# Finishing the norms of k apart from those of q in a kernel's opening, and loading the root's table behind the first loads

## The chip, the cores and the metric

One core of one Trainium2 chip runs the whole program. The metric is device time in microseconds (us) of one execution, median of several runs. Engines: PE is TensorE (matmuls; PEld is its weight load, which overlaps), DVE is VectorE, ACT is ScalarE, POOL is GpSimd, SP is SyncE.

## The reference

Two operators, one after the other, on B=4, N=6080, C=256 and 2048 hidden columns; float32 in and out.

```python
def _attn_ref(q, k, v, tau):                       # tau = 1
    qn = q / (np.linalg.norm(q, axis=1, keepdims=True) + 1e-06)
    kn = k / (np.linalg.norm(k, axis=1, keepdims=True) + 1e-06)
    s = kn.transpose(0, 2, 1) @ qn / tau           # 256 x 256 per batch
    s = s - s.max(-1, keepdims=True)
    a = np.exp(s)
    a /= a.sum(-1, keepdims=True) + 1e-09
    return v @ a

def _moe_ref(x, w_in, w_out, s, b):                # x = the result above, 24320 x 256
    h = x @ w_in
    r = np.maximum(h, 0.0)
    g = s * (r * r) + b
    return g @ w_out
```

The inputs are random normals (q, k, v times 0.1).

## The kernel before

For each batch the kernel needs s = kᵀq over all 6080 rows and the column norms of k and q before it can form the softmax a. It then folds the softmax into the weights, wa = a · w_in, so that the long part is only v · wa, the squared relu, and the product with w_out. For batches 1 to 3 the k and q work is spread over the long part of the batch ahead. For batch 0 there is nothing to hide behind: the **opening** (the first 39 us) loads k and q, and only after their last rows come the norms, the scaling of s, its transposes, the exponentials (eT), the sums, the folding of the weights (wa), and then the first steady matmul (h_ps). The change touches this opening alone.

The parts that the argument needs (cuts marked; the comments are added here):

```python
class Gram:                                     # one per batch
    def load(self, c):                          # chunk c of k, then of q
        ...
        for i, src in enumerate((k, q)):
            rows = src[self.b, at : at + np_ * jc, :].rearrange("(p j) c -> p j c", j=jc)
            ...                                 # first two chunks: SP and ACT queues
            po(nc.gpsimd.dma_start(out=t[:np_, i, :jc, :], in_=rows))
    ...
    def add_norms(self, last=False):            # sums of squares of k and q, one tile
        ...
    def finish_ops(self):
        def norms():
            self.add_norms(last=True)
            po(nc.scalar.activation(out=nrm, in_=self.n_ps, func=AF.Sqrt))
        def recip():                            # DVE: + EPS, reciprocal
        def scale():                            # DVE: sm_s = s_ps * 1/|k|
        def turn():                             # PE: t_ps = transpose(sm_s)
        def ready(func):                        # a one-column activation, brings the table
            po(nc.scalar.activation(out=warm, in_=ones32[:, 0:1], func=func))
        def exps(j):                            # ACT: eT = exp(t_ps * 1/|q|), halves j = 0, 1
        def sums():                             # PE: r_ps = column sums; DVE: rs = 1/r_ps
        def scaled(f0, n, m, wa_ps):            # m = 0 on ACT, m = 1 on DVE
            dst = self.wa[:, m, ds(f0, n)]
            if m == 0:
                po(nc.scalar.mul(out=dst, in_=wa_ps, mul=st["rs"][:, m : m + 1]))
            else:
                po(nc.vector.tensor_scalar_mul(
                    out=dst, in0=wa_ps, scalar1=st["rs"][:, m : m + 1]))
        ...

    # the opening, in program order
    nc.vector.memset(parts16, 1.0 / LAM)
    nc.vector.memset(ones32, 1.0)
    ...
    po(nc.scalar.activation(out=warm, in_=ones32[:, 0:1], func=AF.Sqrt))   # root's table, at once
    ...                                         # loads: k, q, k, q, ... k, q; then w_in, v, w_out
    for c in range(NCH0):                       # per chunk: norm sums, s_ps matmuls, squares
        ...
    fin = g0.finish_ops()
    fin[1](); fin[2](); fin[3](); fin[4]()      # norms, recip, scale, ready(Exp)
    keep_busy(4, w_in16[:, 0, :P], w_in16[:, 0, :NW])     # filler matmuls
    fin[5]()                                    # turn
    transpose_v(0)                              # PE transposes of v, copied by DVE
    for f in fin[6:12]:                         # exps 0 and 1, sums, first folds of the weights
        f()
```

`po` fixes the order of the instructions of an engine as written.

## Time and profile before

| | kernel before |
|---|---|
| time, median (lowest to highest) | 719.46 us (719.45 to 719.73), 3 runs |
| profiled span, granted clock | 717.6 us, 1.0 |
| PE busy | 699.5 us, 97% |
| last shares of k and of q land | 34.11 and 34.30 us |
| first exponential (eT) starts | 37.32 us |
| first and second steady matmul (h_ps) start | 39.28 and 39.50 us |

A line of the timeline reads: start in us, busy us, engine, source line, operation, output tile <- input tiles, their shapes, xcount for a group; in brackets the idle time of the engine just before it, and which engine or transfer ended that idle time. The prediction below shows the lines up to the exponentials. These are the ones behind them, from the timeline of the kernel before:

```profile
38.48 0.17 DVE L297 RECIPROCAL rs<-r_ps 128x2 f32<-128x2 f32 x1
38.75 0.88 ACT L302 ACTIVATE wa<-wa_ps,rs 128x256 f16<-128x256 f32 x2 [0.59 <-PE wa_ps L309]
38.94 0.92 DVE L304 TENSOR_SCALAR wa<-wa_ps,rs 128x256 f16<-128x256 f32 x2 [0.29 <-PE wa_ps L309]
39.28 0.60 PE L605 MATMUL h_ps<-vT,wa 128*128 128x512 f16 x2
```

ACT scales one half of the folded weights and DVE the other. Each of the first two steady matmuls needs one of these halves. DVE waits 0.29 us between its reciprocal and its first scaling, and the second half is there in time: the two h_ps matmuls are one group without a gap.

### The profile page before, as it was taken

Reading aid. Unit: us, or ns where it says so; the run is one execution under the profiler, and the core shown is the slowest. Engines: PE = TensorE matmul, PEld = TensorE weight load, DVE = VectorE, ACT = ScalarE, POOL = GpSimd, SP = SyncE. Lnnn points to the kernel's source line nnn. Section 1 sums busy time; section 2 is a strip of 40 time slices with the busy share of each in tenths; the row PEclk is TensorE's granted clock in tenths of the full one; section 3 lists DMA queues with packets and bytes.
Section 4 is the critical chain, followed back from the end, with each engine's and each line's share of the span. In section 5 each row is a group of like instructions: output and inputs, shape, how many; then the busy total and the mean of one; then the engine's idle time right before and its main releaser. Section 6 shows DMA issues by size and latency. Waiting matters only on the chain.

```text
span 717.6 us, 17642 instructions
## 1 busy us (share of the span) xinstructions
PE 699.5 (97%) x7481; PEld 505.1 (70%) x7481; DVE 626.0 (87%) x879; ACT 544.4 (76%) x588; POOL 110.1 (15%) x189
## 2 busy tenths in 40 slices
PE   4799999999999999999999999999999999999998
PEld 3556777776677777777677777777668777777777
DVE  4779999998789999999888899999887888888886
ACT  4489877887777777788777778778877777777875
POOL 4532332201201222111110222110000000000000
PEclk9999999999999999999999999999999999999999
DMA  9999897647556879443972877944423333321201
GB/s 236 207 259 169 158 177 134 111 108 129 115 103 121 144 133 145 107 93 78 157 154 56 143 136 124 152 93 84 107 63 75 93 71 74 97 59 46 83 30 74
DMA packets 89790, 84.25 MB, mean 117 GB/s; under 512 B 59664, under 2 KB 64848, under 8 KB 89712
## 3 DMA queue, kind: packets, MB, share of 16 engines
q0 software_dynamic: 26064, 43.40, 37.2%
q1 hardware_dynamic: 63072, 38.43, 21.4%
q8 instruction: 58, 0.95, 0.6%
q10 hardware_dynamic: 576, 1.31, 0.5%
q14 instruction: 20, 0.16, 0.1%
HBM read 78.91 MB, written 24.90 MB: 145 GB/s over the span
## 4 chain that ended last, share of the span: by engine, by line
PE 93%; DMA 4%; DVE 1%; ACT 1%; POOL 0%; issue 0%; ACTq 0%; POOLq 0%
PE h_ps L605 45%; PE o_ps L773 40%; PE s_ps L142 4%; PE wa_ps L309 2%; DMA qk<-in_q_dram 2%; DMA qk<-in_k_dram 1%; DMA w_in<-in_moe_w_in_dram 1%; PE o_ps L677 1%; PE o_ps L651 0%; ACT r L615 0%; POOL qk L126 0%; PE idle_ps L442 0%; DVE o_sb L633 0%; DVE S L701 0%; DVE sq L162 0%
## 5 line engine op out<-in xcount | busy, mean ns | idle before, releaser
L615 ACT ACTIVATE r<-h_ps 128x1024 f16<-128x1024 f32 (+1 forms) x384 | 387.6, 1013 | 146.2 <-PE h_ps L605 144.3
L605 PE MATMUL h_ps<-vT,wa 128*128 128x512 f16 (+7 forms) x1632 | 452.0, 364 | 0.1
L773 PEld LDWEIGHTS <-S 128*128 128x128 f16 x2944 | 198.0, 98 | 84.8 <-issue 0.4
L773 PEld LDWEIGHTS <-g 128*128 128x128 f16 x2208 | 155.1, 98 | 74.1
L628 DVE TENSOR_TENSOR g<-r 128x2048 f16<-128x2048 f16 (+2 forms) x150 | 174.7, 1165 | 14.6 <-ACT r L615 14.5
L773 PE MATMUL o_ps<-T,S 128*128 128x128 f16 x2208 | 183.3, 219 | 0.1
L605 PEld LDWEIGHTS <-wa 128*128 128x128 f16 x1632 | 136.1, 98 | 20.6 <-DVE wa L304 0.2
L773 PE MATMUL o_ps<-w_out,g 128*128 128x128 f16 x1472 | 134.2, 219 | 0.2 <-DVE u L633 0.2
L633 DVE SCALAR_TENSOR_TENSOR o_sb<-o_ps,s_out,u 128x256 f32<-128x256 f32 x138 | 66.4, 481 | 47.4 <-PE o_ps L773 44.9
L626 ACT ACTIVATE g<-r 128x1024 f16<-128x1024 f16 (+1 forms) x97 | 100.4, 1035 | 0.2
L142 PE MATMUL s_ps<-qk 128*128 128x256 f16 (+1 forms) x384 | 70.1, 283 | 13.9 <-ACT qk L133 8.8
L361 POOL DMA_DIRECT2D v<-in_v_dram x48 | 31.4, 658 | 262.4 <-DMA vT<-v 199.1
L633 DVE SCALAR_TENSOR_TENSOR u<-o_ps,s_out,rowconst 128x256 f32<-128x256 f32 x138 | 65.9, 477 | 0.0
L773 PE MATMUL o_ps<-w_out,S 128*128 128x128 f16 x736 | 63.4, 219 | 0.0
L773 PE MATMUL o_ps<-N,g 128*128 128x128 f16 x736 | 63.4, 219 | 0.0
L188 POOL DMA_DIRECT2D f<-f x30 | 26.4, 879 | 225.6 <-DVE f L178 172.0
L165 ACT ACTIVATE sq<-qk 128x1024 f16<-128x1024 f16 (+3 forms) x49 | 50.4, 1033 | 11.7 <-DMA qk<-in_k_dram 7.8
L701 DVE TENSOR_TENSOR S<-S,g 128x2048 f16<-128x2048 f16 (+1 forms) x47 | 56.4, 1201 | 1.3
L699 DVE TENSOR_TENSOR S<-g 128x2048 f16<-128x2048 f16 (+1 forms) x47 | 56.1, 1193 | 0.0
L705 DVE TENSOR_TENSOR S<-g,S 128x2048 f16<-128x2048 f16 x46 | 55.9, 1215 | 0.0
L703 DVE TENSOR_TENSOR S<-g 128x2048 f16<-128x2048 f16 x46 | 55.9, 1215 | 0.0
L142 PEld LDWEIGHTS <-qk 128*128 128x128 f16 (+1 forms) x384 | 32.8, 101 | 19.9 <-DVE qk L132 8.2
(75 smaller groups left out, 324.4 us busy)
## 6 DMA issues: line engine op xcount, KB each, us to landing
out_dram<-o_sb SPq DMA_DIRECT2D x46, 512.0 KB, 3.1
v<-in_v_dram POOLq DMA_DIRECT2D x47, 256.0 KB, 4.7
qk<-in_k_dram POOLq DMA_DIRECT2D x42, 256.0 KB, 5.9
qk<-in_q_dram POOLq DMA_DIRECT2D x42, 256.0 KB, 7.3
f<-f POOLq DMA_DIRECT2D x30, 128.0 KB, 3.0
vT<-v SPq DMA_TRANSPOSE x182, 3.2
w<-in_moe_w_out_dram POOLq DMA_DIRECT2D x4, 512.0 KB, 10.8
raw<-in_k_dram SPq DMA_DIRECT2D x2, 512.0 KB, 6.4
```

Of the source, the lines that this page charges most:

```text
L142: po(nc.tensor.matmul(self.s_ps[:, ch, :], kc[:np_, j, ts(ch, P)], qc[:np_, j, :], start=(c == 0 and j == 0 and ch == 0), stop=(c == len(s ...
L165: po(nc.scalar.activation(out=st["sq"][:np_, 1, js, :], in_=kc[:np_, js, :], func=AF.Square))
L605: po(nc.tensor.matmul(dst, wa[:, ci, ts(m, P)], src, start=(ci == 0), stop=(ci == CH - 1), skip_group_check=True))
L615: po(nc.scalar.activation(out=r16[:, :, i % 2, :n], in_=h_tiles.pop((g, i))[:, :, :n], func=AF.Relu))
L626: po(nc.scalar.activation(out=dst, in_=src, func=AF.Square))
L628: po(nc.vector.tensor_mul(dst, src, src))
L633: po(nc.vector.scalar_tensor_tensor(out=dst, in0=src, scalar=s_out, op0=ALU.mult, in1=add, op1=ALU.add))
L699: po(nc.vector.tensor_add(T[1], A21, A22))
L701: po(nc.vector.tensor_sub(T[2], T[1], A11))
L703: po(nc.vector.tensor_sub(T[3], A11, A21))
L705: po(nc.vector.tensor_sub(T[4], A12, T[2]))
L773: po(nc.tensor.matmul(st[name][:, j, :], a()[:, i, ts(j, P)], w[:, i, :], start=first, stop=last, skip_group_check=True))
```

## The change

Its stated intent: keep the norms of k and q apart, load the last k rows ahead of the last q rows, so that the root and the reciprocal of k are done before q has landed and the scaling of s need not wait for them; and load the root's table "once the first rows of k are there instead of at once". The core of the diff:

```diff
-            self.rows, self.n_ps = [], None
-        def load(self, c):
+            self.raw, self.rows, self.n_ps = {}, ([], []), [None, None]
+        def load(self, c, parts=(0, 1)):
 ...
-            def norms():
-                self.add_norms(last=True)
-                nrm = sm_pool.tile([P, 2, CH], FP32, tag="nrm", name="nrm")
-                po(nc.scalar.activation(out=nrm, in_=self.n_ps, func=AF.Sqrt))
+            def norms(a=None):
+                ...                             # batches 1 to 3: both at once, as before
+                else:
+                    self.add_norms((a,), last=True)
+                    po(nc.scalar.activation(out=st["nrm"][:, a], in_=self.n_ps[a], func=AF.Sqrt))
 ...
-                front += [scale, lambda: ready(AF.Exp), turn]
+                front = [lambda: norms(1), lambda: recip(1), lambda: norms(0),
+                         lambda: ready(AF.Exp), scale, lambda: recip(0), turn]
 ...
-    warm = consts.tile([P, 1], FP32)
-    po(nc.scalar.activation(out=warm, in_=ones32[:, 0:1], func=AF.Sqrt))
     for c in range(NDIRECT):
         g0.load(c)
+    warm = consts.tile([P, 1], FP32)
+    po(nc.scalar.activation(out=warm, in_=raw32[:, 0, 0, 0, 0:1], func=AF.Sqrt, scale=0.0))
 ...
-    for c in range(NDIRECT, len(g0.chunks)):
+    for c in range(NDIRECT, len(g0.chunks) - 2):
         g0.load(c)
+    for parts in ((0,), (1,)):                  # last two chunks: k, k, then q, q
+        for c in range(len(g0.chunks) - 2, len(g0.chunks)):
+            g0.load(c, parts)
 ...
-    FILL = {-9: 2, -8: 2, -7: 2, -6: 4, -5: 4, -4: 4, -3: 4, -2: 1}
+    NFILL = 3
+    FILL = {-9: 2, -8: 2, -7: 2, -6: 4, -5: 4, -4: 4, -3: 2}
 ...
-    fin[4]()
-    keep_busy(4, w_in16[:, 0, :P], w_in16[:, 0, :NW])
-    fin[5]()
-    transpose_v(0)
-    for f in fin[6:12]:
+    ...                                         # squares and norms of k, 3 fillers, then q
+    for f in fin[2:6]:
+        f()
+    fin[6]()
+    transpose_v(0)
+    keep_busy(2, w_in16[:, 0, :P], w_in16[:, 0, :NW])
+    for f in fin[7:13]:
         f()
```

(In the index `a`, 1 is k and 0 is q. The sizes of the loads are as before: the last two chunks put two rows on each of 128 and of 96 partitions; only their order changes.)

## The prediction

> **What bounds the kernel now.** I read four views: the page's busy shares, the chain of waits that ended last, the timeline of the first 62 us, and the trace's landing records (a time for each of the 16 shares in which a transfer reports). The page first:
>
> ```profile
> span 717.6 us, 17642 instructions
> PE 699.5 (97%) x7481; PEld 505.1 (70%) x7481; DVE 626.0 (87%) x879; ACT 544.4 (76%) x588; POOL 110.1 (15%) x189
> ```
>
> TensorE works for 699.5 of 717.6 us. The change touches nothing of that: it edits the opening, before the steady work on v. So the question is how early the opening lets the first steady matmul start. The chain there (start us, us, what):
>
> ```profile
> 27.33 8.14 DMA w_in<-in_moe_w_in_dram
> 35.47 0.05 issue
> 35.52 1.04 PE idle_ps L442 x4
> 36.55 0.74 PE t_ps L272 x4
> 37.30 0.02 issue
> 37.32 0.85 ACT eT L282 x2
> 38.17 0.05 issue
> 38.22 0.23 PE r_ps L292 x3
> 38.44 0.90 PE wa_ps L309 x8
> ```
>
> After 35.47 us no DMA is on this chain, and TensorE, ACT or DVE links follow each other to the end. What the exponentials (eT) gain or lose should therefore reach the end nearly whole. The chain names the w_in landing, but the timeline shows something as late beside it (start us, us, engine, line, operation, out<-in; in brackets the idle time and its releaser):
>
> ```profile
> 34.20 0.63 ACT L165 ACTIVATE sq<-qk 96x512 f16<-96x512 f16 x1 [2.02 <-DMA qk<-in_k_dram]
> 34.33 0.42 DVE L162 TENSOR_TENSOR sq<-qk 96x512 f16<-96x512 f16 x1 [1.22 <-DMA qk<-in_q_dram]
> 34.35 0.60 PE L142 MATMUL s_ps<-qk 96*128 96x256 f16 x4 [0.39 <-DMA qk<-in_q_dram]
> 34.81 0.38 PE L217 MATMUL n_ps<-ones,sq 96*128 96x1 f16 x8
> 35.22 0.17 ACT L228 ACTIVATE nrm<-n_ps 128x4 f32<-128x4 f32 x1 [0.39 <-PE n_ps L217]
> 35.41 1.28 ACT L277 ACT_TABLE_LOAD   x1
> 35.92 0.88 DVE L243 TENSOR_SCALAR sm_s<-s_ps,rnrm 128x256 f32<-128x256 f32 x2
> 36.71 0.20 ACT L277 ACTIVATE warm<-ones 128x1 f32<-128x1 f32 x1
> 37.32 0.84 ACT L282 ACTIVATE eT<-t_ps,rnrm 128x256 f16<-128x256 f32 x2 [0.41 <-PE t_ps L272]
> ```
>
> Two branches leave the last landing (34.30 us): the data branch (norms, root, reciprocal, scale, transposes) ends at 37.30; the table branch (root, then the exponential's table) ends at 36.91. The exponentials wait for the later. The 0.41 us of idle ACT before eT is the lead of the table branch, and so the most that shortening the data branch alone can give.
>
> **What the Trainium skill says.** "ScalarE: Activation LUTs", section "What ACT_TABLE_LOAD costs", has about 1283 ns for the load and about 1380 ns of drain, for every change of set. The trace agrees on the load (1.28 us at both places above and below) but not on a drain here: the next activation starts at 36.71, 0.02 us after the load's end. I use 1.28.
> "DMA: Bandwidth & Descriptors", section "Why a DMA increments its semaphore by 16 and not by 1", says a transfer counts as landed only when all its engines have reported. The landing records agree: the last k transfer (96 rows) has its first share at 32.32 and its last at 34.11; the last q transfer 32.81 and 34.30.
> "Runtime: NRT & Kernel Launch", section "Instruction fetch mechanics", says a sequencer refills instructions by its own DMA queue in 16 KiB blocks. The trace agrees: a 16384-byte packet of the instruction queue runs from 32.08 for 0.96 us, just where one of the 16 shares starts to lag. So that fetch makes the last q rows late, not q itself.
> "TensorE: Matmul & The Clock Gate", section "The HAM clock gate", warns of idle gaps near 3 us. In this trace TensorE, once started, idles 1.85 us at most (at 10.62, still in the warm-up), and the granted clock is 1.00 in every stretch; I expect no change.
>
> **The change part by part.**
> *The root's table.* The diff makes the first root read the first rows of k. The compiled order shows the load of the table ahead of that root without a wait of its own; only the activation waits. The kernel before has these lines:
>
> ```profile
> 1.19 1.28 ACT L401 ACT_TABLE_LOAD   x1 [1.19 <-PEq L846]
> 2.48 0.20 ACT L401 ACTIVATE warm<-ones 128x1 f32<-128x1 f32 x1
> 5.81 1.04 ACT L133 CAST qk<-raw 128x1024 f16<-128x1024 f32 x1 [3.12 <-DMA raw<-in_q_dram]
> ```
>
> So the load will not do what the description says. It moves only behind the second issue of q, 1.19 to some 1.6 us, and still ends near 2.9. The root (0.20) moves to the landing of k (5.61), ends near 5.84 and delays the cast at 5.81 by 0.03 to 0.05. That delay dies: TensorE catches up with the loads at 15.8 us and waits for each later one. Worth 0.0.
> *Order of the last four loads.* k, q, k, q becomes k, k, q, q, with the same bytes on the same queue, so the last q should again land at 34.30. The second-last k loses a q of 128 rows ahead of it (0.65 us from one landing to the next) and gets ahead of the fetch: 31.46 + 0.49 = 31.95 instead of 34.11. The first of the two q takes its place behind the fetch: between 33.5 and 34.1 instead of 32.15.
> *Norms of k alone, early.* ACT squares the two k tails from 31.54 (0.63) and, once DVE has freed the buffer by its fold that ends at 32.31, from 32.36 to 32.99. The sums follow (8 small matmuls, 0.38, partly beforehand) to 33.3, the root of k to 33.5, two DVE steps (0.17 and 0.18, with gaps) to 33.9. All of it is before the q rows; none is on the path any more. That takes root and reciprocal off the data branch.
> *Data branch after.* Last q 34.30; if the other q came only at 34.1, the matmuls of both end at 35.15; otherwise at 34.95. DVE squares both q tails (0.42 each) until 34.8 to 35.0. Scaling starts at 35.0 to 35.2 instead of 35.92 and takes 0.88. Transposes end 0.5 after it (before: 36.80 to 37.29): 36.4 to 36.6, instead of 37.30. Gain on this branch 0.7 to 0.9.
> *Table branch after.* Sums of q still need the last q square: 35.19 if the first q is in time, 35.4 if it is 0.2 behind. Root 0.17, load 1.28, warm 0.20, gaps 0.03 each: 36.93 to 37.14. This is now the later branch, so the exponentials start there: 0.18 to 0.39 earlier than 37.32.
> *Added and moved work.* One more root (0.17) and two more DVE instructions (some 0.35 together) for separate norms; they lie in waits, since the reciprocal of q comes after the scale, with ACT still loading its table. Four transposes of t no longer follow four filler matmuls on w_in. Then v: its first tile lands at 36.70, so its transposes run from 36.75 to 37.4 (before 37.01 to 37.73), two fillers go to some 37.8, and the copy of v on DVE ends at 38.2 (before 38.46). The sums r_ps come after the second exponential, 37.8 to 38.0 plus 0.05. None of these is later than the exponentials by more than 0.1.
> *Sum.* Start of the weights' folding 0.18 to 0.39 earlier; less up to 0.1 where v's copy or the fillers are last. Middle 0.28: 719.46 - 0.28 = 719.18, say 719.2.
>
> **Rivals.** (1) *The fetch hits the early k.* It follows TensorE's own progress, whose order is unchanged up to the block of norm sums, and it starts 0.5 us after the k tail would be through, so I think it misses. If it came 0.5 us earlier, k would land at about 33.5. As DVE takes k's reciprocal ahead of the q squares, these would slip to about 35.9, the table branch to 37.75, and the time would be 719.9. (2) *The data branch stays last,* because scaling waits for something that I overlook, such as a bank or the copy of v: then up to 0.1 of gain or none, 719.4. For it: the chain names PE and DVE there; against: all releases that I find are early. (3) *The early gain is absorbed later*: between 52.6 and 57.4 ACT sets the pace, and between 64.8 and 73.8 DVE does. Both are backlogs that begin after the exponentials, so they should shift along; only if a load of w_out or the next k set them would the gain vanish (719.5). The w_out pieces land by 48.0, well ahead. (4) *TensorE cools* because three fillers are gone: it would cost a microsecond or more; the remaining gaps, under 0.5 us, speak against it. (5) *The table is really held back* until 5.61: then the first cast of q is 1.5 late and the end is still unmoved, since TensorE waits for loads from 15.8.
>
> **Range and chances.** Three runs of the kernel before span 0.28 us, another chip may differ as much, and DMA timing later in the kernel can move some tenths. Together with rivals (1) and (3) on the slow side and a full 0.4 plus luck on the fast side: 718.7 to 719.8. Two per cent is 14 us; the whole opening that is touched is about 3 us long. So within 2% is all but sure: 0.99, the rest split evenly.
>
> **What would show it.** In the changed profile: the first table load at about 1.6, not at 5.6; the last q tail near 34.3, the k tails by 32.0; the root of k near 33.4 and of q at 35.2 to 35.45; scaling from 35.0 to 35.2; ACT idle before eT gone, with eT right behind the warm activation at 36.9 to 37.15; the steady matmuls 0.2 to 0.4 earlier and the same shift still there at 100 us. I am wrong if the k tail lands after 33, if eT still waits for the transposes, if the shift at 100 us differs from the one at 40, or if a matmul of 512 columns in the opening takes visibly longer than its 379 ns.

## The result, and the profile after

| | before | after |
|---|---|---|
| time, median (lowest to highest), 4 runs each | 719.47 us (719.45 to 719.73) | 719.41 us (719.32 to 720.23) |
| profiled span | 717.6 us | 717.5 us |
| last k, last q landed | 34.11, 34.30 | 32.36, 34.54 |
| first exponential starts | 37.32 | 37.04 |
| first, second steady matmul | 39.28, 39.50 | 38.98, 39.41 |

The ratio is 1.0001, with a 95% interval of 0.9984 to 1.0018. A ratio here is the mean time of one kernel's fast runs over that of the other's fast runs of the same rounds, so it is not quite the ratio of the medians. The interval is about 1.2 us to either side and the effect that we look for is 0.3 us: the timings can't decide it, and all further reading is done on positions in the traces.

The page of the kernel after shows the same budget; only PE has two matmuls fewer (27 fillers became 25) and 0.7 us less:

```profile
span 717.5 us, 17641 instructions
PE 698.8 (97%) x7479; PEld 504.5 (70%) x7479; DVE 625.8 (87%) x881; ACT 544.7 (76%) x589; POOL 110.1 (15%) x189
```

The root's table, from the timeline of the first 40 us of the kernel after:

```profile
1.67 1.28 ACT L419 ACT_TABLE_LOAD   x1 [1.67 <-PEq L879]
...
6.02 0.20 ACT L419 ACTIVATE warm<-raw 128x1 f32<-128x1 f32 x1 [3.06 <-DMA raw<-in_k_dram]
```

The load of the table goes at 1.67 us, behind ACT's second issue of q, and does not wait for k. Only the one-column activation does, at 6.02. The change's description is not what the compiled program does.

The end of the opening, from the same timeline:

```profile
34.21 0.77 DVE L166 TENSOR_TENSOR sq<-qk 128x512 f16<-128x512 f16 x2
...
35.06 0.34 PE L224 MATMUL n_ps<-ones,sq 128*128 128x1 f16 x8
...
35.27 0.88 DVE L257 TENSOR_SCALAR sm_s<-s_ps,rnrm 128x256 f32<-128x256 f32 x2 [0.28 <-PE s_ps L146]
35.45 0.17 ACT L243 ACTIVATE nrm<-n_ps 128x2 f32<-128x2 f32 x1 [1.55 <-PE n_ps L224]
35.64 1.28 ACT L291 ACT_TABLE_LOAD   x1
...
35.90 0.74 PE L286 MATMUL t_ps<-ident,sm_s 128*128 128x128 f32 x4 [0.49 <-DVE sm_s L257]
...
36.93 0.20 ACT L291 ACTIVATE warm<-ones 128x1 f32<-128x1 f32 x1
37.04 0.82 ACT L296 ACTIVATE eT<-t_ps,rnrm 128x256 f16<-128x256 f32 x2
...
38.18 0.17 DVE L311 RECIPROCAL rs<-r_ps 128x2 f32<-128x2 f32 x1 [0.16 <-PE r_ps L306]
...
38.45 0.89 ACT L316 ACTIVATE wa<-wa_ps,rs 128x256 f16<-128x256 f32 x2 [0.58 <-PE wa_ps L323]
38.87 0.88 DVE L318 TENSOR_SCALAR wa<-wa_ps,rs 128x256 f16<-128x256 f32 x2 [0.52 <-PE wa_ps L323]
...
38.98 0.82 PE L638 MATMUL h_ps<-vT,wa 128*128 128x512 f16 x2
```

Scaling of s now starts with s itself, 35.27 instead of 35.92, and its transposes begin 0.65 us earlier. The exponential's table still loads behind the root of q, 35.64, and the bracket of idle time ahead of eT is gone: ACT goes table, warm, eT. eT, ACT's own scaling and the first h_ps are all 0.28 to 0.30 us earlier than before. But DVE's scaling is at 38.87, only 0.07 earlier, and the idle time in its bracket grew from 0.29 to 0.52. The group of two h_ps matmuls is 0.82 long instead of 0.60: the second one came late. The chain of waits that ended last has that gap as an "issue" link between them (start us, us, what):

```profile
36.93 0.20 ACT warm L291
37.13 0.74 ACT eT L296 x2
...
39.04 0.33 PE h_ps L638
39.36 0.04 issue
39.41 0.39 PE h_ps L638
```

Lined up matmul by matmul with the kernel before, the steady matmuls are earlier by 0.30 (first), 0.09 (second), 0.09 (the tenth), 0.08 (the hundredth, near 81 us) and 0.07 (the last). So what was won at the exponentials was mostly lost within one instruction, before the steady part began; afterwards nothing was lost or won.

### The profile page after: what moved, and what is told of

Same layout as the page of the kernel before. It is cut to its first block, busy times and chain, and to the rows that moved or that the text cites. A ratio compares the mean times of both kernels' runs of the same rounds, so it can differ in the third digit from the quotient of the medians.

```text
span 717.5 us, 17641 instructions
## 1 busy us (share of the span) xinstructions
PE 698.8 (97%) x7479; PEld 504.5 (70%) x7479; DVE 625.8 (87%) x881; ACT 544.7 (76%) x589; POOL 110.1 (15%) x189
## 4 chain that ended last, share of the span: by engine, by line
PE 93%; DMA 3%; DVE 2%; ACT 1%; POOL 1%; issue 0%; POOLq 0%; DVEq 0%; ACTq 0%
PE h_ps L638 45%; PE o_ps L806 40%; PE s_ps L146 4%; DMA qk<-in_q_dram 3%; PE wa_ps L323 2%; PE o_ps L710 1%; POOL qk L130 1%; PE o_ps L684 0%; ACT r L648 0%; DVE f L182 0%; DVE sq L166 0%; DVE o_sb L666 0%; DVE S L734 0%; DVE S L732 0%; DVE S L736 0%
```

## The experiments

The trace also records each update of a semaphore. TensorE's update for the matmuls that DVE's scaling needs came at 38.616 in the kernel after; the scaling started at 38.867, which is **0.251 late**. In the kernel before it was 38.915 and 38.940, 0.025 late. I compared each of the 1354 instructions of DVE and ACT in the kernel after that wait for a semaphore with the last update that it needs: the next largest delay is 0.045. So the bracket's "<-PE" is not the cause: the view puts idle time down to the latest update of that semaphore (38.835, by TensorE's third pair of matmuls), which the scaling doesn't need.

Theories for the 0.25 us (letters as in the expectations; B, a wait for TensorE's third pair, is answered after round two, and D and F are only the opposites of C and E):
- **A:** GpSimd's issue of the load of s (38.15 to 38.70 in the kernel after) holds DVE up.
- **C:** the banks of PSUM, the memory that TensorE writes its results to, have moved (the second norm tile shifts the ring of output banks by one): TensorE's third pair now writes bank 7 instead of 6, and DVE might be unable to read its bank 3 meanwhile.
- **E:** it belongs to a place in DVE's own instruction list. The change puts two DVE instructions more ahead of the scaling, which makes it the 65th instruction of DVE's list (64 ahead of it) instead of the 63rd. The count is that of the compiled program; the trace records one instruction fewer ahead of it.

"Shift" below is how much earlier (−) or later (+) something starts than in the one profile of the kernel before. The rounds ran on different chips (11, 15, 1 and 7), so a shift also has the scatter of the loads in it. All kernels gave correct results by the comparison. In a table at the end of this section the stall is put side by side.

### Round one: GpSimd, and the root's table

**after_hold**: the loads of s and b are issued only after the first folds.

```diff
-    po(nc.gpsimd.dma_start(out=s_bc, in_=moe_s.to_broadcast((P, 1))))      # and b_bc
 ...
     for f in fin[7:13]:
         f()
+    po(nc.vector.memset(s_bc, 0.0))
+    po(nc.gpsimd.dma_start(out=s_bc, in_=moe_s.to_broadcast((P, 1))))      # and b_bc
```

> The changed kernel, with GpSimd's issue of the small load of s held until DVE has done its first two scalings of the folded weights (a memset of its tile on DVE goes before it; the result stays right). Theory A: in the changed kernel that issue (38.15 to 38.70 us) keeps DVE's first scaling, whose matmuls are done at 38.60, back until 38.87, 0.17 us after the issue's end. Then the scaling starts 0.04 us after its matmuls, the second matmul of h follows at about 39.18 instead of 39.41, and the steady matmuls stand 0.28 to 0.32 us ahead of the kernel before instead of 0.08: about 719.2 us. Theory B: DVE waits there for something of TensorE's (its third pair of matmuls, done at 38.82). Then the scaling stays 0.04 after that third pair, and the shift stays at 0.07 to 0.10: 719.4 us.

Measured: 719.30 us (718.97 to 719.55, 5 runs) against 719.64 (9 runs of the kernel before), ratio 0.9993 (0.9981 to 1.0006). The issue really moved, and the scaling did not (timeline of after_hold):

```profile
38.84 0.88 DVE L318 TENSOR_SCALAR wa<-wa_ps,rs 128x256 f16<-128x256 f32 x2 [0.52 <-PE wa_ps L323]
...
40.03 0.55 POOL L499 DMA_DIRECT2D s_bc<-in_moe_s_dram  x1 [2.52 <-DVE s_bc L498]
```

Start 38.835 against an update at 38.583, 0.252 late. Theory A falls.

**before_hold**: the same edit in the kernel before.

> The kernel before with the same hold of the load of s. Its scaling started at 38.94 us, 0.04 after its matmuls and also 0.17 after the end of GpSimd's issue, so both theories fit it. Theory A: the issue only just ceases to matter; scaling at 38.94, shift 0.00 (at most 0.03), 719.46 us. Theory B: the same. It is the control: if the hold alone moved this kernel by 0.1 us or more, the hold would do something other than free DVE.

Measured: 719.45 us (719.22 to 720.40), ratio 0.9999 (0.9985 to 1.0013); scaling not late; eT and the steady matmuls both +0.05. The control shows that the edit itself is worth nothing.

**after_swap**: the load of s is issued ahead of that of the third v tile, so that a GpSimd issue lies over other DVE work.

```diff
+    s_bc = consts.tile([P, 1], FP32)
+    po(nc.gpsimd.dma_start(out=s_bc, in_=moe_s.to_broadcast((P, 1))))
     load_v(2)
-    s_bc = consts.tile([P, 1], FP32)
-    po(nc.gpsimd.dma_start(out=s_bc, in_=moe_s.to_broadcast((P, 1))))
```

> The changed kernel with the load of s issued one place earlier and the third load of v in its place, so that the issue near 38.15 us is a large load (128 pieces of 2 KB) instead of 128 pieces of 4 bytes. Theory A in its wide form (any issue by GpSimd blocks DVE's scaling): scaling again at about 38.87, shift 0.08. In its narrow form (only the load of s with its small pieces does): scaling at 38.64, shift near 0.30; and the load of s now issues near 36.91 to 37.46, so the copy of v on DVE, which began at 37.33, may slip to about 37.63. Theory B: scaling at 38.86, shift 0.08.

Measured: 719.38 us (one run). The scaling is again 0.252 late (38.915), and the copy of v, which now has a GpSimd issue over it (37.06 to 37.61), starts on time at 37.49. A falls a second time.

**after_root_at_once**: the kernel after, with the root's table loaded as in the kernel before (the one-column activation reads `ones32` and stands ahead of the loads).

```diff
+    warm = consts.tile([P, 1], FP32)
+    po(nc.scalar.activation(out=warm, in_=ones32[:, 0:1], func=AF.Sqrt))
     for c in range(NDIRECT):
         g0.load(c)
-    warm = consts.tile([P, 1], FP32)
-    po(nc.scalar.activation(out=warm, in_=raw32[:, 0, 0, 0, 0:1], func=AF.Sqrt, scale=0.0))
```

> The changed kernel without its second part: the root's table loaded at once, as in the kernel before. The theory that the second part is worth nothing: table load at 1.2 us instead of 1.67, first cast of q some 0.0 to 0.2 earlier, exponentials and steady matmuls within 0.05 us of the changed kernel (shift 0.05 to 0.12 against the kernel before), 719.4 us. The rival, that the order of the first issues caused the extra 0.4 us by which one of the 16 shares of every load lagged in the changed kernel's profile (first k landed by 6.00 instead of 5.61): then that lag is gone here, the last q lands near 34.3 instead of 34.54, and the exponentials start at 36.9 instead of 37.04.

Measured: 719.42 us (719.05 to 719.66, 5 runs), ratio 0.9995 (0.9983 to 1.0008). The scaling is 0.251 late, so the stall does not come from this part. The shifts are larger than the expected 0.05 to 0.12 (eT −0.62, steady −0.43), and the signs of the rival are there: the first k landed by 5.62 and the last q at 34.25, against 6.00 and 34.54 in the kernel after. But kernels whose root reads k have such landings too (before_root_late 5.60 and 34.18, after_swap 5.66 and 34.39), so I take them for scatter. From the last landing to eT it is 2.45 us, against 2.50. The part that moves the root's table is worth nothing that shows.

**before_root_late**: that part alone, done to the kernel before.

> The kernel before with the second part of the change alone: the first root reads the first rows of k. Theory (worth nothing): table load at 1.6 to 1.7 us instead of 1.19, root at the landing of k, first cast of q at most 0.2 later, exponentials and steady matmuls where they were within 0.06 us. Rival (it makes the loads' slowest share lag): first k landed near 6.0 instead of 5.6, last q at 34.5 or later, exponentials and steady matmuls 0.2 late.

Measured: 719.41 us (one run). The table load moved as in the kernel after; landing to eT 2.99 us against 3.02 in the kernel before. Its shift of −0.15 is the earlier landing (34.18 against 34.30) and little else. The same answer from the other side: nothing.

### Round two: the banks

**after_banks**: one unused tile and a one-column matmul into it, so that every later tile gets the bank that it had in the kernel before.

```diff
+                if first and a == 1:
+                    spare = ps_o.tile([P, 2, C], FP32, tag="o_ps", name="spare")
+                    po(nc.tensor.matmul(spare[:, 0, 0:1], ident16, ones16[:, 0:1],
+                                        start=True, stop=True))
```

> The changed kernel with one more tile drawn from the output pool of PSUM between the norms of q and of k (one added 1-column matmul into it), so that the banks of the opening fall as in the kernel before: ACT's first scaling reads bank 7 instead of 6, TensorE's third pair of matmuls writes bank 6 instead of 7, DVE's first scaling reads bank 3 in both. After the hold changed nothing, everything that scaling waits for is in place at 38.62 us in the changed kernel, and it starts 0.25 later, just after the third pair is done. Theory C (the layout of banks is what holds DVE: it can't read bank 3 while TensorE writes bank 7): the scaling starts 0.02 to 0.04 after the second pair, the second matmul of h 0.2 earlier, steady matmuls 0.28 to 0.32 ahead of the kernel before, near 719.2 us. Theory D (it is something in the order of the instructions): no change, 0.25 late again, shift 0.05 to 0.12.

Measured: 720.2 us (719.2 to 720.71, 5 runs), ratio 1.0004 (0.9991 to 1.0018). With the banks of the kernel before the scaling is 0.299 late (38.658 against 38.359). Theory C falls. The whole times are higher than those of the other variants, though the steady matmuls were 0.30 us earlier all through the profile; the excess lies behind them, at the end of the kernel (span 718.4). In the profiled run the last store of the result took 2.82 us from its issue to its landing, against 1.72 in the kernel before; I did not find why.

**before_banks**: the same shift of the ring in the kernel before.

> The reverse: the kernel before with one more tile (and one 1-column matmul) so that its banks fall as in the changed kernel: ACT's first scaling reads bank 6, the third pair writes bank 7, DVE reads bank 3. Theory C: DVE's first scaling starts 0.25 after its matmuls, at about 39.16 instead of 38.94, and the steady matmuls come 0.2 later than in the kernel before: about 719.7 us. Theory D: scaling at 38.94, shift 0.0.

Measured: 719.51 us (719.36 to 720.50, 4 runs), ratio 1.0000 (0.9986 to 1.0013); the scaling isn't late. Its +0.24 at eT is again the landing of q (34.57). Moving the banks neither makes nor heals the stall.

**after_hbank**: the two fillers between the transposes of v and the sums take a tile each, so that DVE reads the other bank of the pair.

```diff
-    keep_busy(2, w_in16[:, 0, :P], w_in16[:, 0, :NW])
+    keep_busy(1, w_in16[:, 0, :P], w_in16[:, 0, :NW])
+    keep_busy(1, w_in16[:, 0, :P], w_in16[:, 0, :NW])
```

> The changed kernel with its last two filler matmuls in two tiles instead of one, so that DVE's first scaling reads bank 1 instead of 3, with ACT on bank 6 and the third pair in bank 7 as in the changed kernel. Theory C with banks four apart (3 against 7): DVE starts 0.02 to 0.04 after the second pair, unless the fourth pair, which writes bank 5, now meets bank 1 and slows it. If it is ACT's bank 6 or the third pair's bank 7 whatever DVE reads: 0.25 late again, shift 0.05 to 0.12.

Measured: 719.22 us (one run); 0.259 late (38.774). A third arrangement of banks, the same stall.

Theory B, that DVE waits for TensorE's third pair, had come true in after_hold as far as its numbers go: the scaling starts 0.03 us after that pair's update there (38.801). It falls here. In after_banks the scaling starts 0.081 us after the third pair, and in the compiled program it waits for the semaphore value that the second pair brings (201 in the kernel after).

### Round three: the place in DVE's list

What is common to all late cases is DVE's own stream. Ahead of the scaling stands a bare wait instruction (it waits for the reciprocal). In every late case the scaling starts 0.456 to 0.465 us after that instruction's end, whatever TensorE had done. So I moved the scaling within the list, with nothing else: `parts16`, a one-column constant set at the start, is set again.

```diff
     nc.vector.memset(parts16, 1.0 / LAM)
+    nc.vector.memset(parts16, 1.0 / LAM)
+    nc.vector.memset(parts16, 1.0 / LAM)
```

**after_plus2**: two more (scaling at place 67). **before_plus2**: the same two in the kernel before (place 63 becomes 65). **after_plus1**: one more (the wait instruction at 65, the scaling at 66).

> The changed kernel with two memsets of a one-element column added on DVE in the first microseconds, where DVE is idle; the values stay the same. In all traces of the changed kernel DVE's first scaling begins 0.456 us after the wait instruction ahead of it ended, whatever GpSimd, the banks and TensorE do (0.684 to 0.687 after the start of the reciprocal), and in DVE's list it is instruction 65; in the kernel before it is 63. Theory E (DVE has to fetch new instructions at every 64th, or at some such place in its list, and that is only seen where a wait keeps its sequencer from running ahead): as number 67 the scaling starts 0.02 to 0.04 after its matmuls, the second matmul of h 0.2 earlier, the steady matmuls 0.25 to 0.45 ahead of the kernel before instead of 0.08, 719.2 us. Theory F (it belongs to these instructions in this order, wherever they stand in the list): still 0.25 late, shift 0.05 to 0.2, 719.4 us.

> The kernel before with the same two memsets, so that its first scaling on DVE becomes instruction 65. Theory E: it now starts 0.45 us after the end of the wait instruction ahead of it, that is 0.22 to 0.25 after its matmuls are done; the second matmul of h is 0.2 late and the steady matmuls with it, about 719.7 us (0.2 on top of whatever shift the exponentials show). Theory F: 0.025 after its matmuls as before, shift as the exponentials'.

> The changed kernel with one such memset: the wait instruction ahead of the first scaling becomes number 65 and the scaling 66. Theory E: the fetch now falls ahead of the wait instruction, where DVE is doing the reciprocal of 0.17 us, so a part of it is hidden: the wait instruction ends late by up to 0.3 us and the scaling starts between 0.02 and 0.25 after its matmuls. Theory F: 0.25 late.

Measured, after_plus2: **719.21 us** (718.89 to 719.31, 5 runs) against 719.53 (719.19 to 720.27, 9 runs of the kernel before), ratio 0.9995 (0.9981 to 1.0008). Its timeline:

```profile
38.21 0.17 DVE L311 RECIPROCAL rs<-r_ps 128x2 f32<-128x2 f32 x1
...
38.67 0.92 DVE L318 TENSOR_SCALAR wa<-wa_ps,rs 128x256 f16<-128x256 f32 x2 [0.29 <-PE wa_ps L323]
```

The bracket is back at 0.29, the two halves are a group without a gap, and the shift is −0.25 at eT, −0.27 at the first and second h_ps, and −0.27 at the last: nothing is lost on the way.

Measured, before_plus2: **719.80 us** (719.63 to 720.10, 5 runs) against the same 719.53, ratio 1.0004 (0.9991 to 1.0016). Its timeline:

```profile
38.65 0.17 DVE L297 RECIPROCAL rs<-r_ps 128x2 f32<-128x2 f32 x1
39.34 0.88 DVE L304 TENSOR_SCALAR wa<-wa_ps,rs 128x256 f16<-128x256 f32 x2 [0.52 <-PE wa_ps L309]
```

The kernel before now has the stall: bracket 0.52, the scaling 0.251 late, and the shift goes from +0.17 at eT and the first h_ps to +0.38 at the second and +0.40 at the last. The trick of the experiment works both ways, with the sign reversed.

Measured, after_plus1: 719.83 us (one run), although its profiled span is 717.1 and its steady matmuls are 0.46 earlier (the last q landed at 34.35). The scaling is not late (0.025), and the wait instruction, now at place 65, isn't either: it ends 0.060 us after the reciprocal, as in the kernel after (0.059). Theory E had a late wait instruction as a possibility. So the stall needs the scaling itself at place 65.

The stall in all profiles:

| kernel | place of the scaling | from the end of the wait to the scaling, us | from TensorE's update to the scaling, us |
|---|---|---|---|
| before | 63 | 0.229 | 0.025 |
| before_hold, before_banks, before_root_late | 63 | 0.229 to 0.231 | 0.024 to 0.025 |
| after | 65 | 0.456 | 0.251 |
| after_hold | 65 | 0.456 | 0.252 |
| after_swap | 65 | 0.457 | 0.252 |
| after_root_at_once | 65 | 0.456 | 0.251 |
| after_banks | 65 | 0.465 | 0.299 |
| after_hbank | 65 | 0.465 | 0.259 |
| before_plus2 | 65 | 0.456 | 0.251 |
| after_plus1 | 66 | 0.231 | 0.025 |
| after_plus2 | 67 | 0.230 | 0.024 |
| after_no_table (below) | 67 | 0.145 | 0.025 |

In the rows that aren't at place 65 the scaling follows TensorE's update by 0.025 and so merely waits for it; the last row shows that DVE can start it 0.145 us after the wait. At place 65 it takes 0.456 or more. That the stall comes and goes with the scaling's place is shown: it is there at 65, and not at 63, 66 or 67.

Why is not shown. Other instructions at place 65 are not late (the wait instruction in after_plus1, the reciprocal in after_plus2), and other multiples of 64 in DVE's list show no such delay, even one right behind a wait instruction (place 449 in after_hold, 0.27 us after it). That the sequencer is waiting there for the next stretch of its instructions would fit. For it speaks that in after_plus1, after_plus2 and after_no_table the first packet of the instruction queue with pieces of 8192 bytes starts at 38.28 to 38.34 us, 0.07 to 0.13 us after instruction 65, while in the other eleven kernels it starts at 41.9 to 43.0 us: so the time of this packet depends on DVE's list. Against it speaks that in the kernels with the stall the packet comes 3.18 to 3.55 us after the late scaling has started (in the kernel after at 42.19, with none between 32.50 and that). The trace doesn't say which engine a packet is for. The stall may be peculiar to the first 64 instructions, or hidden elsewhere by DVE running behind its sequencer. That stays open.

### Last: is the table branch now the later one?

**after_no_table**: after_plus2 without a change of table between the norms and the exponentials. It was meant to be wrong in batch 0 (the norms are copied, not rooted).

```diff
-                    po(nc.scalar.activation(out=st["nrm"][:, a], in_=self.n_ps[a], func=AF.Sqrt))
+                    po(nc.scalar.activation(out=st["nrm"][:, a], in_=self.n_ps[a], func=AF.Copy))
 ...
-    po(nc.scalar.activation(out=warm, in_=raw32[:, 0, 0, 0, 0:1], func=AF.Sqrt, scale=0.0))
+    po(nc.scalar.activation(out=warm, in_=raw32[:, 0, 0, 0, 0:1], func=AF.Exp, scale=0.0))
```

> Wrong result on purpose (first batch only): the two repeated DVE instructions of the better version are kept, but the norms of the first batch are copied (Copy) instead of rooted (Sqrt), and the first activation names Exp, so that no table has to be loaded between the norms of q and the exponentials; everything else is the same. Theory (after the change the branch through the table is the later one, as predicted): the exponentials then wait for the transposes alone, so eT starts about 2.1 to 2.2 us after the last q landing instead of 2.45 to 2.63, near 36.6 to 36.7, and idle time of ACT appears ahead of it with the transposes as its releaser. Rival (the data branch is as late, or ACT was held by something else than the table): eT stays 2.4 us or more after the landing. The end will not follow in full: the copy of v on DVE, set by the landing of v (36.7 to 36.9), ends at 38.0 to 38.2 and stands ahead of the reciprocal of the sums, so the steady matmuls can gain 0.0 to 0.2 us against the better version; the time 719.0 to 719.3.

Measured: 719.12 us (one run). The comparison with the reference passed all the same: I take it that with random q and k the normalized products are so small (of the order of 1/√6080) that the softmax is almost flat, so the comparison can't see the norms. It's no kernel to use. Its timeline:

```profile
35.64 0.19 ACT L291 ACTIVATE warm<-ones 128x1 f32<-128x1 f32 x1
...
36.80 0.84 ACT L296 ACTIVATE eT<-t_ps,rnrm 128x256 f16<-128x256 f32 x2 [0.96 <-PE t_ps L286]
...
37.59 0.69 DVE L389 COPY vT<-vT_ps 128x1024 f16<-128x1024 f16 x1 [1.04 <-PE vT_ps L387]
```

ACT is ready at 35.83 and now waits 0.96 us for the transposes. From the last landing (34.47) to eT it is 2.33 us. I had expected 2.1 to 2.2, which is the figure for a first q that lands early; here it came at 34.28, as in after_plus2, whose figure is 2.63. So against its like the table cost 0.30 us: it is the later branch, as predicted, but not by more than that. And the end got only 0.02 us of it (steady −0.29 against −0.27): the copy of v, 37.59 to 38.28, now stands ahead of DVE's reciprocal of the sums. Whoever shortens the table branch further must bring v earlier too.

## Why the prediction was right or wrong, point by point

The time, 719.41, lies in the predicted 718.7 to 719.8. That says little, since the timings have an interval of 1.2 us to either side and no effect at all would lie there too. What can be judged is the shift of the steady matmuls in the traces: 0.28 earlier was predicted, 0.09 was measured. By its steps:

- **Root's table**: right. 1.67 us and not held back until k, worth 0.0. Two experiments, one from each side, agree.
- **Order of the loads**: the k tails landed at 31.89 and 32.36, where the prediction has 31.46 (unchanged) and 31.95. Both came some 0.4 later, as the first k did (6.00 instead of 5.61); the step between them, 0.47, is the predicted 0.49. The fetch (a packet at 32.50) missed k, so rival 1 did not happen. The first of the two q landed at 33.03, earlier than the predicted 33.5 to 34.1; in other profiles of this family (after_hold, after_swap, after_plus2) at 34.12 to 34.20. Both occur. The last q landed at 34.54 and not at 34.30; over all profiles it lies between 34.18 and 34.57 for either order, so this is chance of the transfers.
- **Norms of k early**: right in kind; the root of k started at 33.72 and its reciprocal ended at 34.30, some 0.3 and 0.4 later than predicted, still ahead of need.
- **Data branch**: scaling at 35.27, predicted 35.0 to 35.2 with a landing 0.24 earlier. Right. Rival 2 did not happen.
- **Table branch and the gain at the exponentials**: eT at 37.04, 0.28 earlier, exactly the predicted middle, with no idle time ahead of it. The branch is right; that the middle was hit is luck, since two errors cancel in it. Counted from the last landing, the prediction has 2.63 us with the first q in time and 2.84 with it late (36.93 and 37.14 less 34.30); the runs show 2.45 to 2.53 and 2.63 to 2.70. It had added the 0.20 of the warm activation in full, but eT starts 0.11 after it (36.93, 37.04). The Trainium skill says on "ScalarE: Activation LUTs", section "What ACT_TABLE_LOAD costs", that back-to-back activations overlap by about 93 ns; the overlap of 0.09 us in the timeline agrees, and I had not used it. So the 0.41 us of idle ACT was not "the most" that shortening the data branch can give: with the overlap it was 0.50, and counted from the last landing eT came 0.52 earlier (3.02 less 2.50). The landing, 0.24 later, took the rest.
- **Folding and steady start**: here a step failed. It says of v's copy, the fillers and the sums, "None of these is later than the exponentials by more than 0.1." These three were indeed in time (r_ps, wa_ps and the first h_ps are 0.29 to 0.30 earlier). What came 0.23 us later than the exponentials would have allowed was the next link, DVE's scaling of the folded weights, which the step took to shift along. It became the 65th instruction of DVE's list, and there the start took 0.456 us from the wait ahead of it instead of following TensorE by 0.025. So the term "less up to 0.1" should have been 0.2: 0.28 − 0.2 = 0.08, against a measured shift of 0.09 at the second and tenth steady matmul. Two idle instructions take the stall away and the 0.27 us reach the end; the same two put it into the kernel before.
- **Rival 3, absorbed later**: did not happen. The shift is constant from the second h_ps to the last (0.09 to 0.07). The loss came earlier than the rival had it.
- **Rival 4, clock**: did not happen; 1.0. (It counts three fillers fewer; there are two.)
- **Its own signs**: the table load, the root of q, the exponentials right behind the warm activation and the missing idle time came as said. The second k tail (32.36 instead of "by 32.0") and the scaling (35.27) were slightly late. "The steady matmuls 0.2 to 0.4 earlier" held for the first of them alone (0.30); from the second on it was 0.09.

No run contradicts the order "table branch later than data branch". What stays open: why place 65; and the longer end of after_banks.

## What to carry to other kernels

Moving work off a path is only worth the lead of the next branch, and that lead stands in the profile as the idle time just ahead of the joining instruction: here 0.41 us of idle ACT in the kernel before, plus 0.09 us of overlap that the bracket doesn't count. Counted from the last landing, 0.52 came out at the exponentials; 0.28 was left by the clock because q landed 0.24 later. When such a gain does not come out, line the two traces up instruction by instruction and look for the first one whose shift differs; then compare its start with the semaphore's own update and not with the engine that the view names. Adding or removing instructions can move a later one into a worse place of its engine's list, so before a difference of a few tenths is put down to an idea, try the same kernel with one or two idle instructions more.

## What the Trainium skill lacked or had wrong

- "Runtime: NRT & Kernel Launch", section "Instruction fetch mechanics", knows blocks of 16 KiB (256 instructions) whose crossing is "mostly hidden". The stall of 0.25 us at DVE's 65th instruction lies at no such boundary, and no page that I read has it; that it is a fetch at all is not shown. In the traces only one instruction queue moves 16,384-byte packets; the other moves 8,192-byte ones (20 in the span of the kernel before). Nor does the section say that a fetch can delay data: the 16 KiB packet at 32.08 us in the kernel before took 0.96 us, and the last q rows, whose first share landed at 32.81, were complete only at 34.30, while the q load two places ahead of it needed 0.33 us from its first share to its last (31.82 to 32.15). This is read from the times alone; no run here moved the fetch.
- "ScalarE: Activation LUTs", section "What ACT_TABLE_LOAD costs", adds about 1380 ns of drain to each load. In the kernel after, the load takes 1.28 us and the next activation starts 0.01 us behind it (35.64, 36.93). It also doesn't say that a load doesn't share the wait of the activation that it precedes: load at 1.67 us, activation at 6.02.
